# Two casts of the first batch's keys move from VectorE to ScalarE in a fused attention and feed-forward kernel

## The chip, the cores and the metric

One core of one Trainium2 chip. The metric is the time of one execution in microseconds of the device (us), the median over runs. The engines are named as the profile names them: PE is TensorE (matmuls; PEld its weight loads), DVE is VectorE, ACT is ScalarE, POOL is GpSimd, SP is SyncE.

## What is computed

```
a       = softmax(phi)                         # over the last axis, 32 memory slots
k_m     = einsum('bhsm,bhsd->bhmd', a, k)      # 32 summary keys for each head
v_m     = einsum('bhsm,bhsd->bhmd', a, v)
attn    = softmax(q @ k_m^T / sqrt(64))
x       = (attn @ v_m), heads side by side     # 4608 tokens x 512
out     = ((x @ w_a) * (x @ w_b)) @ w_out      # 512 -> 1536 -> 512, float32
```

There are 8 batches of 576 tokens with 8 heads of 64; all inputs and the output are float32. Inside, nearly everything is float16 with float32 sums.

## The kernel before

**Work of one batch.** The keys, values and queries of a batch come as a tile of 128 partitions by 4 head pairs by 576 columns. Exp of phi (ScalarE, L301) is the weight with which TensorE sums keys and values over the tokens (L387 for batch 0, L333 for the others). VectorE scales these sums, TensorE transposes them, and VectorE copies them out as `kvT`. Scores are products of `kvT` with VectorE's 32x32 transposes of the queries (L310, or L316 for batch 1). ScalarE takes exp of them, and sums, logarithm and exp again give the normalised attention `A`.

**Folding.** The values are not multiplied with `A` first. TensorE multiplies the summary values with columns of w_a and w_b (a fold, L526). VectorE or ScalarE copies the result out of PSUM into `vab` (a fold copy, L558). An up-projection is then one product of `vab` with `A` over 256 rows, two matmuls (L738): `a` gives x @ w_a, copied by ScalarE or VectorE (L742), and `b` gives x @ w_b, which VectorE multiplies with it into `ht` (L745). The down-projections of token blocks (L665) follow, in seven products instead of eight.

**The order.** No scheduler places the work. A list of units, `PLAN`, is written out by hand, and each engine gets its instructions in the order in which the units are listed. Each engine works through its own queue in that order and waits by semaphores for the others. The names in the list: `0ks1` are batch 0's key sums of the second half of the heads; `0hv0b` is a fold of batch 0 with a half chunk (256 columns) of w_b, and `0hx0b1` the copy of its second group; `0v1a` is a fold with a whole chunk of 512 columns of w_a; `a0.3.1` is product a of batch 0, output rows 3, second half of the tokens, and `b0.3.1` its partner; `1exp1` is exp of half of batch 1's phi; `1qh10` is a transpose of part of batch 1's queries; `1kv` are batch 1's key and value sums; `2km1` is VectorE's scaling of one group of such sums; `d3` takes the next three steps of the down-projection, a step being one matmul with what belongs to it; `wb512:1024` issues the load of these columns of w_b; `F4` are four filling matmuls on zeros.

**Transfers.** All inputs but one go through GpSimd's queue, which also converts them to float16 on the way. The exception is batch 0's keys. They come as float32 through the queues of SyncE and ScalarE, half each, into room that the tile `ht` lends:

```
L182  k_f32 = ht[:, 0:4].bitcast(F32)
L183  halves = [slice(0, 2), slice(2, 4)]
L184  for engine, x in zip((nc.sync, nc.scalar), halves):
L185      engine.dma_start(out=k_f32[:, x], in_=rows(k, 0)[:, x])
L186  nc.scalar.preload_act_table_set("natural_log_exp_and_others")
```

Two casts, L234 and L235, bring them to float16 in `kv_sb`, each 128 partitions by 1152 columns. They stand ahead of all units of the list. The fold copies of batch 0's half chunks are all VectorE's; this choice and the return of the PSUM bank are here:

```
L553  def take_fold(lo, hi, z, gs=range(2), other=False):
L554      first, second = (x != other for x in (b == 0 and hi <= 512, b < 2))
...
L559          banks.free(bank)
```

Of the kernel before, what the change touches and what calls it, by code (L numbers as in the profile page):

```python
# [17 lines left out]
PLAN = """  # L18
0exp1 F2 wa0:256 wb0:256 wa256:512 F1 M 0ks1 O 0qt1 0kt1 0qt0 wb256:512 0exp0 0ks0 0kt0 0s0 0e0 0qt3 0qt2 0s1 0e1
0den00 p1 0vs0 0den01 0nr00 0den11 0nr11 0den10 0nr10 F1 0vs1 0nr01 0vt0 0vt1 0hv0b 0hx0b0 0hv1a 0hv1b 0hx1b0 0hx1b1  # L20
v1 0hx0b1 0hv0a 0hx1a1 F4 0hx1a0 a0.3.1 1exp1 0hx0a1 a0.2.1 0hx0a0 a0.0.1 b0.0.1 c0.1.0 1exp0 b0.2.1 c0.3.0 b0.3.1
b0.3.0 b0.1.0 c0.0.0 a0.2.0 b0.2.0 b0.0.0 a0.1.1 k1 1kv 1km1 F1 1km0 b0.1.1 1kvt wa512:1024 0v1a 0x1a1 0x1a0 q1.0
1qh10 1qh20 wb512:1024 1qh00 1v1a 1x1a0 1x1a1 1v0a 1v0b a0.4.0 1x0b0 q1.1 1qh30 a0.6.1 a0.6.0 1x0a1 1x0a0 1x0b1
wa1024:1536 1sh0 wb1024:1536 1eh00 0v1b 1eh10 0x1b1 0x1b0 1v1b 1x1b1 1den00 1den10 o0 a0.5.1 b0.4.0 o3 b0.6.0 1qh01
1nr00 1nr10 a0.5.0 a0.7.1 b0.5.0 b0.7.1 1qh31 1x1b0 b0.6.1 a0.4.1 a0.7.0 b0.4.1 a1.2.0 b0.7.0 1qh21 a1.3.0 b1.2.0
a1.4.0 1qh11 a1.1.0 o1 b0.5.1 b1.1.0 a1.0.0 1sh1 1eh01 o4 1eh11 b1.3.0 b1.4.0 o5 0v2a 0x2a0 0x2a1 o2 0v2b a1.6.0 0x2b1
a1.5.0 b1.5.0 0x2b0 1v2a k2 1x2a1 p2 1v2b 1y2b1 a1.7.0 v2 1x2b0 g0.3 b1.6.0 1x2a0 p3 b1.0.0 a0.11.0 c0.10.0 d2 b1.7.0
a0.8.0 b0.8.0 q2 1den01 b0.10.0 b0.11.0 a0.11.1 b0.11.1 T20 1nr01 1den11 V00 a1.9.0 1nr11 a0.9.0 b0.9.0 g0.0 d1
a0.10.1 a0.8.1 a1.11.0 b0.10.1 d1 b1.11.0 a1.5.1 b1.9.0 b1.5.1 b0.8.1 a1.11.1 T10 b1.11.1 d2 T21 a1.10.0 a1.8.0 k3
a0.9.1 v3 b1.8.0 b1.10.0 a1.0.1 b1.0.1 2exp0 a1.6.1 b0.9.1 a1.2.1 V01 a1.1.1 b1.6.1 g0.1 a1.4.1 a1.7.1 b1.4.1 2exp1  # L30
b1.2.1 d3 a1.3.1 V11 T30 d6 2kv d1 g0.2 d2 T31 g1.0 d3 2km1 2km0 d8 a1.10.1 b1.3.1 2kvt d3 3exp0 3exp1 a1.8.1 b1.1.1
2v0a 2x0a1 2qt2 2x0a0 2qt3 2qt0 2qt1 2v1b 2x1b1 2x1b0 g1.1 d7 q3 p5 g1.2 d7 g2.0 q4 d2 2sc d2 2e1 d3 2e0 c1.9.1 b1.9.1
d3 b1.8.1 2den1 d3 h1.3 h2.1 2den0 2nr0 d4 2v1a 2v2b 2x2b1 2y2b0 3kv 3km1 2nr1 d6 3km0 d7 2x1a0 d1 2x1a1 d1 b1.7.1
2v2a v5 2x2a0 2v0b 3qt2 2x0b0 2x0b1 b1.10.1 d2 g2.2 a2.0.0 a2.6.0 b2.6.0 d1 k5 3qt3 2x2a1 d3 3qt1 a2.7.0 a2.2.0 b2.0.0
a2.4.0 d6 v4 d2 3kvt 5exp0 b2.7.0 d2 3qt0 d4 a2.3.0 b2.2.0 3sc 3e0 d2 b2.3.0 3e1 d6 3den0 3nr0 g2.3 a2.1.0 d3 b2.4.0
d3 b2.1.0 a2.5.0 b2.5.0 a2.5.1 a2.8.0 p4 d3 a2.1.1 d3 5exp1 3den1 g4.3 d1 b2.1.1 b2.8.0 a2.9.0 d1 k4 d1 a2.10.1 b2.9.0
a2.4.1 q5 b2.10.1 3nr1 4qt2 3v0b 3v0a 3x0a0 3x0b0 5kv p6 h3.3 b2.5.1 a2.10.0 3x0a1 d2 a2.11.0 a2.9.1 d2 b2.10.0 d1
h3.0 h3.1 h3.2 b2.11.0 b2.9.1 4qt3 d2 3x0b1 a2.0.1 b2.0.1 a2.11.1 b2.4.1 b2.11.1 a2.7.1 b2.7.1 a2.8.1 a2.3.1 a2.2.1
b2.2.1 d2 a3.2.0 a3.3.0 d2 4exp0 b3.2.0 d1 b2.8.1 b3.3.0 d4 4qt1 4exp1 d6 3v2a 3x2a1 4kv 4km1 d5 4km0 3x2a0 a3.0.0 d10
b2.3.1 d1 4qt0 4kvt a2.6.1 b2.6.1 h4.0 a3.3.1 d4 6exp1 d2 5km1 d4 4sc 4e1 d3 4e0 5km0 a3.1.0 h4.1 b3.3.1 d4 a3.0.1  # L40
b3.1.0 h4.2 4ed 4sm0 d1 a3.1.1 d2 5qt0 d1 3v1b 3x1b0 q6 3v2b 3x2b1 5qt1 3v1a d11 3x1a0 d1 b3.0.0 d7 3x1b1 b3.0.1
# [39 lines left out]
def kernel(  # L81
# [11 lines left out]
    nc = tc.nc  # L93
# [51 lines left out]
    kvs = [kv_sbs[b % 2] for b in range(B)]  # L145
# [36 lines left out]
    k_f32 = ht[:, 0:4].bitcast(F32)  # L182
# [49 lines left out]
    make_identity(nc, ident)  # L232
    nc.vector.memset(kv_sbs[0][:, 2], 1.0 / CS)
    for x in halves:  # L234
        nc.vector.tensor_copy(out=kvs[0][:, 0, x], in_=k_f32[:, x])  # L235
    turn = {}

    def tt(engine, **operands):
# [616 lines left out]
```

## Time and profile before

| | us |
|---|---|
| median of three runs | 237.22 |
| lowest and highest | 237.01, 237.41 |
| the profiled execution | 236.62 |
| its span, first to last instruction | 234.70 |
| TensorE busy | 216.0 |
| VectorE busy | 199.3 |
| ScalarE busy | 168.8 |
| GpSimd busy | 148.3 |

The mean granted clock of TensorE over the span is 0.993. A row of the timeline gives the start in us from the span's start, the time in us, the engine (with a q behind it: the queue that issues a transfer), the line, the operation, the tile written and the tiles read, and how many instructions were merged; in brackets stands how long the engine had been idle and what released it. A row of groups gives the form and the count, then busy us and the mean ns of one, then the idle time ahead. A row of issues gives KB and the us from issue to landing. A row of windows gives the stretch, then for each engine busy us and the number of instructions, then granted clock, share of the transfer engines, and GB/s.

### The profile page before, as it was taken

Reading aid. Unit: us, or ns where it says so; the run is one execution under the profiler, and the core shown is the slowest. Engines: PE = TensorE matmul, PEld = TensorE weight load, DVE = VectorE, ACT = ScalarE, POOL = GpSimd, SP = SyncE. Lnnn points to the kernel's source line nnn. Section 1 sums busy time; section 2 is a strip of 40 time slices with the busy share of each in tenths; the row PEclk is TensorE's granted clock in tenths of the full one; section 3 lists DMA queues with packets and bytes.
Section 4 is the critical chain, followed back from the end, with each engine's and each line's share of the span. In section 5 each row is a group of like instructions: output and inputs, shape, how many; then the busy total and the mean of one; then the engine's idle time right before and its main releaser. Section 6 shows DMA issues by size and latency. Waiting matters only on the chain.

```text
span 234.7 us, 7495 instructions
## 1 busy us (share of the span) xinstructions
PE 216.0 (92%) x2906; PEld 164.6 (70%) x2906; DVE 199.3 (85%) x514; ACT 168.8 (72%) x445; POOL 148.3 (63%) x147
## 2 busy tenths in 40 slices
PE   2177989999899999999999999999999999999993
PEld 0133646588587778877777787887778868788882
DVE  3756799999978757789987999998999999999962
ACT  2224459987699998697987988877898679666330
POOL 7685232647785379995867499599474981772201
PEclk9999799999999999999999999999999999999999
DMA  6999999999999999399927632121303213122164
GB/s 229 237 197 258 205 205 205 206 261 256 194 250 217 228 219 245 112 198 253 235 31 164 100 93 67 25 52 43 88 7 89 56 38 91 24 70 67 25 160 110
DMA packets 26259, 34.09 MB, mean 145 GB/s; under 512 B 2000, under 2 KB 20304, under 8 KB 26224
## 3 DMA queue, kind: packets, MB, share of 16 engines
q0 software_dynamic: 19760, 23.14, 54.1%
q1 hardware_dynamic: 5952, 9.70, 15.7%
q10 hardware_dynamic: 512, 0.79, 1.0%
q8 instruction: 22, 0.36, 0.6%
q14 instruction: 13, 0.11, 0.1%
HBM read 42.47 MB, written 9.44 MB: 221 GB/s over the span
## 4 chain that ended last, share of the span: by engine, by line
PE 84%; DVE 9%; ACT 2%; DMA 2%; issue 1%; DVEq 0%
PE py L665 20%; PE pb L738 14%; PE pa L738 14%; PE pv L665 10%; PE pva L526 5%; PE py L761 5%; PE px L665 5%; PE pv L761 3%; DMA ht<-in_k_dram 2%; DVE kv_sb L235 2%; PE pkv L333 2%; DVE vab L558 1%; PE pscore L422 1%; DVE ht L745 1%; PE px L761 1%; PE pk L387 1%
## 5 line engine op out<-in xcount | busy, mean ns | idle before, releaser
L745 DVE TENSOR_TENSOR ht<-a_sb,pb 128x288 f16<-128x288 f16 (+2 forms) x144 | 60.5, 444 | 11.6 <-ACT a_sb L742 4.3
L738 PEld LDWEIGHTS <-vab 128*128 128x128 f16 x576 | 55.9, 99 | 16.2 <-issue 2.2
L742 ACT CAST a_sb<-pa 128x288 f16<-128x288 f32 (+2 forms) x139 | 53.9, 416 | 18.5 <-PE pa L738 15.3
L738 PE MATMUL pa<-A,vab 128*128 128x288 f16 (+2 forms) x288 | 55.2, 290 | 0.5 <-DVE vab L558 0.4
L738 PE MATMUL pb<-A,vab 128*128 128x288 f16 (+2 forms) x288 | 55.0, 287 | 0.1
L558 ACT CAST vab<-pva 128x512 f16<-128x512 f32 x82 | 45.8, 611 | 4.8 <-PE pva L526 4.5
L665 PEld LDWEIGHTS <-h_sums 128*128 128x128 f16 x432 | 41.3, 98 | 9.2 <-issue 2.0
L665 PEld LDWEIGHTS <-ht 128*128 128x128 f16 x324 | 31.3, 98 | 7.3 <-issue 2.1
L665 PE MATMUL py<-w_sums,h_sums 128*128 128x256 f16 x216 | 35.5, 273 | 0.0
L665 PE MATMUL pv<-wo_sb,h_sums 128*128 128x256 f16 x216 | 34.5, 273 | 0.0
L240 POOL TENSOR_TENSOR h_sums<-ht 128x768 f16<-128x768 f16 x17 | 27.7, 1642 | 8.1 <-DVE ht L745 3.7
L766 ACT COPY z<-py 128x288 f32<-128x288 f32 x48 | 19.4, 416 | 6.5 <-PE py L761 4.6
L240 POOL TENSOR_TENSOR ht<-ah,bh 128x288 f16<-128x288 f16 x20 | 14.3, 731 | 11.8 <-DVE ah L770 8.7
L665 PE MATMUL py<-wo_sb,ht 128*128 128x256 f16 x108 | 18.4, 273 | 0.0
L665 PE MATMUL px<-wo_sb,ht 128*128 128x256 f16 x108 | 18.3, 273 | 0.0
L665 PE MATMUL py<-w_sums,ht 128*128 128x256 f16 x108 | 17.8, 273 | 0.0
L672 ACT ACTIVATE u<-py 128x256 f32<-128x256 f32 x36 | 14.6, 404 | 4.5 <-PE py L665 4.0
L435 ACT ACTIVATE E<-pscore 128x288 f16<-128x288 f32 x28 | 9.6, 418 | 7.7 <-PE pscore L422 7.5
L240 POOL TENSOR_TENSOR h_sums<-h_sums,ht 128x768 f16<-128x768 f16 x8 | 13.1, 1640 | 3.1 <-DVE h_sums L240 2.7
L301 ACT ACTIVATE exp_sb<-phi_sb 128x576 f16<-128x576 f32 x16 | 10.8, 694 | 5.2 <-DMA phi_sb<-in_phi_dram 5.2
L240 POOL TENSOR_TENSOR h_sums<-ht,h_sums 128x768 f16<-128x768 f16 x8 | 13.1, 1643 | 0.2
L761 PE MATMUL py<-asum,vab 128*128 128x288 f16 x48 | 13.1, 286 | 0.0
(107 smaller groups left out, 401.8 us busy)
## 6 DMA issues: line engine op xcount, KB each, us to landing
out_dram<-o_sb SPq DMA_DIRECT2D x68, 128.0 KB, 2.4
phi_sb<-in_phi_dram POOLq DMA_DIRECT2D x8, 576.0 KB, 8.0
kv_sb<-in_v_dram POOLq DMA_DIRECT2D x8, 576.0 KB, 9.9
kv_sb<-in_k_dram POOLq DMA_DIRECT2D x7, 576.0 KB, 10.7
q_sb<-in_q_dram POOLq DMA_DIRECT2D x6, 576.0 KB, 9.6
wo_sb<-in_moe_w_out_dram POOLq DMA_DIRECT2D x6, 256.0 KB, 14.0
wa_sb<-in_moe_w_a_dram POOLq DMA_DIRECT2D x2, 512.0 KB, 15.4
wb_sb<-in_moe_w_b_dram POOLq DMA_DIRECT2D x2, 512.0 KB, 17.4
```

The costliest lines, as they stand in the source:

```text
L240: x = engine.tensor_tensor(**operands)
L301: nc.scalar.activation(out=t["exp"][:, 2 * z:2 * z + 2, :, :], in_=phis[b][:, 2 * z:2 * z + 2, :].rearrange("p c (i m) -> p c i m", m=M), ...
L435: nc.scalar.activation(out=Ev[:, g, :, z, :], in_=pss, func=AF.Exp, scale=1.0 / (8.0 * CS))
L526: nc.tensor.matmul(t["pva", lo, z][g][0][32 * j:32 * j + 32, 0:hi - lo], t["kvT"][64 * r:64 * r + 64, 4 + g if side else 2, M * j:M * j + ...
L558: engine_copy(out=vabs[b][z][:, g, lo:hi], in_=pva[:, 0:hi - lo])
L665: nc.tensor.matmul(po, lhs[:, i], rhs[:, i], start=first and i == 0, stop=i == KH - 1, skip_group_check=not first)
L672: nc.scalar.mul(out=x, in_=po, mul=scale)
L738: nc.tensor.matmul(ps, vabs[b][x][:, g, P * i:P * (i + 1)], attn[b][:, g, ts], start=(g == 0), stop=(g == 1))
L742: engine_copy(out=a_sbs[b, i, hf][:, :n], in_=ps)
L745: nc.vector.tensor_tensor(out=ht[:, i, t0:t0 + n], in0=a_sbs.pop((b, i, hf))[:, :n], in1=ps, op=ALU.mult)
L761: nc.tensor.matmul(x[bank][0], lhs, rhs, start=first, stop=True, skip_group_check=True)
L766: engine_copy(out=x[name], in_=po)
```

## The change

The two casts of batch 0's keys become ScalarE copies. In ScalarE's queue they stand behind the table load and ahead of the two exp instructions of batch 0. On VectorE nothing stands in their place.

Three units of the list are at another place: `0hx0b1` from ahead of `0hv0a` to behind `1exp1`, so behind `a0.3.1`; `a1.1.0` from behind `1qh11` to ahead of `a1.3.0`; `2km1` one step of the down-projection forward. The other changed lines of the list only break elsewhere. On the engines this gives: ScalarE two instructions more and VectorE two fewer at the start, one fold copy two places further back on VectorE, and two matmuls of `a1.1.0` six matmuls further ahead on TensorE. GpSimd and SyncE keep their order.

```
-v1 0hx0b1 0hv0a 0hx1a1 F4 0hx1a0 a0.3.1 1exp1 0hx0a1 a0.2.1 0hx0a0 a0.0.1 b0.0.1
+v1 0hv0a 0hx1a1 F4 0hx1a0 a0.3.1 1exp1 0hx0b1 0hx0a1 a0.2.1 0hx0a0 a0.0.1 b0.0.1
...
-1qh21 a1.3.0 b1.2.0 a1.4.0 1qh11 a1.1.0 o1
+1qh21 a1.1.0 a1.3.0 b1.2.0 a1.4.0 1qh11 o1
...
-g1.0 d3 2km1 2km0 d8
+g1.0 d2 2km1 d1 2km0 d8
...
     for x in halves:
-        nc.vector.tensor_copy(out=kvs[0][:, 0, x], in_=k_f32[:, x])
+        nc.scalar.copy(out=kvs[0][:, 0, x], in_=k_f32[:, x])
```

More of the change, by code (lines that the diff above doesn't have):

```diff
@@ L20 @@
 0den00 p1 0vs0 0den01 0nr00 0den11 0nr11 0den10 0nr10 F1 0vs1 0nr01 0vt0 0vt1 0hv0b 0hx0b0 0hv1a 0hv1b 0hx1b0 0hx1b1
-v1 0hx0b1 0hv0a 0hx1a1 F4 0hx1a0 a0.3.1 1exp1 0hx0a1 a0.2.1 0hx0a0 a0.0.1 b0.0.1 c0.1.0 1exp0 b0.2.1 c0.3.0 b0.3.1
+v1 0hv0a 0hx1a1 F4 0hx1a0 a0.3.1 1exp1 0hx0b1 0hx0a1 a0.2.1 0hx0a0 a0.0.1 b0.0.1 c0.1.0 1exp0 b0.2.1 c0.3.0 b0.3.1
 b0.3.0 b0.1.0 c0.0.0 a0.2.0 b0.2.0 b0.0.0 a0.1.1 k1 1kv 1km1 F1 1km0 b0.1.1 1kvt wa512:1024 0v1a 0x1a1 0x1a0 q1.0
@@ L24 @@
 wa1024:1536 1sh0 wb1024:1536 1eh00 0v1b 1eh10 0x1b1 0x1b0 1v1b 1x1b1 1den00 1den10 o0 a0.5.1 b0.4.0 o3 b0.6.0 1qh01
-1nr00 1nr10 a0.5.0 a0.7.1 b0.5.0 b0.7.1 1qh31 1x1b0 b0.6.1 a0.4.1 a0.7.0 b0.4.1 a1.2.0 b0.7.0 1qh21 a1.3.0 b1.2.0
-a1.4.0 1qh11 a1.1.0 o1 b0.5.1 b1.1.0 a1.0.0 1sh1 1eh01 o4 1eh11 b1.3.0 b1.4.0 o5 0v2a 0x2a0 0x2a1 o2 0v2b a1.6.0 0x2b1
+1nr00 1nr10 a0.5.0 a0.7.1 b0.5.0 b0.7.1 1qh31 1x1b0 b0.6.1 a0.4.1 a0.7.0 b0.4.1 a1.2.0 b0.7.0 1qh21 a1.1.0 a1.3.0
+b1.2.0 a1.4.0 1qh11 o1 b0.5.1 b1.1.0 a1.0.0 1sh1 1eh01 o4 1eh11 b1.3.0 b1.4.0 o5 0v2a 0x2a0 0x2a1 o2 0v2b a1.6.0 0x2b1
 a1.5.0 b1.5.0 0x2b0 1v2a k2 1x2a1 p2 1v2b 1y2b1 a1.7.0 v2 1x2b0 g0.3 b1.6.0 1x2a0 p3 b1.0.0 a0.11.0 c0.10.0 d2 b1.7.0
@@ L30 @@
 a0.9.1 v3 b1.8.0 b1.10.0 a1.0.1 b1.0.1 2exp0 a1.6.1 b0.9.1 a1.2.1 V01 a1.1.1 b1.6.1 g0.1 a1.4.1 a1.7.1 b1.4.1 2exp1
[L31 to L38, printed above, removed]
+b1.2.1 d3 a1.3.1 V11 T30 d6 2kv d1 g0.2 d2 T31 g1.0 d2 2km1 d1 2km0 d8 a1.10.1 b1.3.1 2kvt d3 3exp0 3exp1 a1.8.1
+b1.1.1 2v0a 2x0a1 2qt2 2x0a0 2qt3 2qt0 2qt1 2v1b 2x1b1 2x1b0 g1.1 d7 q3 p5 g1.2 d7 g2.0 q4 d2 2sc d2 2e1 d3 2e0 c1.9.1
+b1.9.1 d3 b1.8.1 2den1 d3 h1.3 h2.1 2den0 2nr0 d4 2v1a 2v2b 2x2b1 2y2b0 3kv 3km1 2nr1 d6 3km0 d7 2x1a0 d1 2x1a1 d1
+b1.7.1 2v2a v5 2x2a0 2v0b 3qt2 2x0b0 2x0b1 b1.10.1 d2 g2.2 a2.0.0 a2.6.0 b2.6.0 d1 k5 3qt3 2x2a1 d3 3qt1 a2.7.0 a2.2.0
+b2.0.0 a2.4.0 d6 v4 d2 3kvt 5exp0 b2.7.0 d2 3qt0 d4 a2.3.0 b2.2.0 3sc 3e0 d2 b2.3.0 3e1 d6 3den0 3nr0 g2.3 a2.1.0 d3
+b2.4.0 d3 b2.1.0 a2.5.0 b2.5.0 a2.5.1 a2.8.0 p4 d3 a2.1.1 d3 5exp1 3den1 g4.3 d1 b2.1.1 b2.8.0 a2.9.0 d1 k4 d1 a2.10.1
+b2.9.0 a2.4.1 q5 b2.10.1 3nr1 4qt2 3v0b 3v0a 3x0a0 3x0b0 5kv p6 h3.3 b2.5.1 a2.10.0 3x0a1 d2 a2.11.0 a2.9.1 d2 b2.10.0
+d1 h3.0 h3.1 h3.2 b2.11.0 b2.9.1 4qt3 d2 3x0b1 a2.0.1 b2.0.1 a2.11.1 b2.4.1 b2.11.1 a2.7.1 b2.7.1 a2.8.1 a2.3.1 a2.2.1
 b2.2.1 d2 a3.2.0 a3.3.0 d2 4exp0 b3.2.0 d1 b2.8.1 b3.3.0 d4 4qt1 4exp1 d6 3v2a 3x2a1 4kv 4km1 d5 4km0 3x2a0 a3.0.0 d10
```

## The prediction

> **What bounds the kernel now.** I read the page first, then the chain of waits of the first 70 us, then the timeline of that stretch engine by engine, the transfers with their landings, and busy time by windows.
>
> ```profile
> span 234.7 us, 7495 instructions
> PE 216.0 (92%) x2906; PEld 164.6 (70%) x2906; DVE 199.3 (85%) x514; ACT 168.8 (72%) x445; POOL 148.3 (63%) x147
> ...
> 36.00:234.70 198.70, 193.60 (x2468) 152.85 (x2466) 175.16 (x456) 155.24 (x413) 127.65 (x116) 1.00 0.63 131
> ```
>
> The last row is busy time after 36 us: TensorE works 193.60 of 198.70 us (97%). From there on it sets the time, it takes its instructions in the order of the list, and whatever its start is moved by, the end is moved by nearly as much. Before 36 us it is 216.0 - 193.6 = 22.4 us busy in 36: that stretch has 13.6 us of idle time. The chain of waits (start, us, what) says what it waited for:
>
> ```profile
> 0.81 4.95 DMA ht<-in_k_dram
> ...
> 5.79 4.64 DVE kv_sb L235 x2
> ...
> 10.57 1.17 PE pk L387 x34
> ...
> 21.86 2.09 DVE vab L558 x6
> ...
> 24.00 0.67 PE pa L738 x2
> ```
>
> Batch 0's keys land at 5.76, two VectorE casts (L235, the instructions that the change moves) take 4.64 us with nothing else on the chain, and 0.14 us later the first sums of keys start (10.57). At 24.00 the first up-projection starts behind six fold copies. The casts are dear because of their neighbour; three rows of the timeline, by engine:
>
> ```profile
> 5.79 2.07 DVE L235 CAST kv_sb<-ht 128x1152 f16<-128x1152 f32 x1 [2.38 <-DMA ht<-in_k_dram]
> 7.78 2.65 DVE L235 CAST kv_sb<-ht 128x1152 f16<-128x1152 f32 x1
> 7.22 2.59 POOL L803 MEMSET kv_sb<- 128x2304 f16 x1
> ```
>
> GpSimd issues transfers until 7.22 and then fills a tile until 9.81. The second cast ends 0.62 us after that fill (10.43), the first 0.64 us after the issues (7.86): each looks like 0.6 us of work behind a wait for GpSimd. The Trainium skill says so (SBUF — State Buffer, "SBUF: two separate sides"): VectorE in its two-port mode and GpSimd hold one port pair in turn, each blocking the other for a whole instruction. These ends agree.
>
> **The casts on ScalarE.** It is free: after its table load it waits for batch 0's phi and does the two halves of exp from 7.81 to 9.07. The casts now stand ahead of those in its queue. No row has ScalarE casting 1152 columns; the nearest, by shape (mean ns of one):
>
> ```profile
> 1.34 1.28 ACT L186 ACT_TABLE_LOAD   x1 [1.34 <-PEq L839]
> ...
> 7.81 1.26 ACT L301 ACTIVATE exp_sb<-phi_sb 128x576 f16<-128x576 f32 x2 [5.19 <-DMA phi_sb<-in_phi_dram]
> ...
> L558 ACT CAST vab<-pva 128x512 f16<-128x512 f32 x82 | 45.8, 611 | 4.8 <-PE pva L526 4.5
> ...
> L486 ACT ACTIVATE vsum<-asum 128x576 f16<-128x576 f32 x4 | 2.8, 688 | 0.1
> L486 ACT ACTIVATE vsum<-asum 128x288 f16<-128x288 f32 x4 | 1.7, 436 | 0.1
> ```
>
> From 288 to 576 columns, same types, same memory, the price grows by 252 ns; 576 columns more make 688 + 504 = 1192 ns. Bounds: twice the 576-column instruction, 1376; the CAST scaled up by columns, 1375; below, the 620 ns that VectorE needs unblocked. I take 1.19, by the row of the same memory. Casts 5.79 + 2.38 = 8.17; the half of exp that comes first 0.68 (half of 1.26 with its overlap, rounded up) to 8.85; plus the 0.14 above: the sums start at 8.99, **1.58 us earlier**. The second half of exp would end at 9.5; its reader, the second sums of keys, would come at 12.64 - 1.58 = 11.06:
>
> ```profile
> 12.64 1.15 PE L387 MATMUL pk<-kv_sb,exp_sb 64*32 64x128 f16 x36
> ```
>
> A rule of the Trainium skill speaks against the change (ScalarE: Activation LUTs, "Rules for kernel authors"): plain elementwise work belongs on VectorE, up to about three times faster per element. By it alone the two casts would cost 1.24 us on VectorE (0.62 each) against 2.38, so the change would lose 1.1 us here; the row of 4.64 us decides against it, since VectorE isn't free of GpSimd.
>
> Moved with it: VectorE has nothing from 3.4 us until the sums are done. GpSimd's two mask instructions wait for a VectorE memset behind those sums, and eight transfer issues stand behind them in its queue; all go some 1.6 us sooner. That brings no data sooner: the 16 DMA engines are full and serve that queue in order.
>
> ```profile
> DMA  6999999999999999399927632121303213122164
> ...
> 12.47 0.31 POOL L270 TENSOR_SCALAR_AFFINE_SELECT ones<-ones 128x128 f16<-128x128 f16 x1 [2.66 <-DVE ones L269]
> ...
> 15.33 0.78 POOL L152 DMA_DIRECT2D kv_sb<-in_k_dram  x1
> 16.06 0.79 POOL L174 DMA_DIRECT2D wa_sb<-in_moe_w_a_dram  x1
> 16.79 0.80 POOL L171 DMA_DIRECT2D q_sb<-in_q_dram  x1
> 17.52 0.81 POOL L174 DMA_DIRECT2D wb_sb<-in_moe_w_b_dram  x1
> ...
> kv_sb<-in_k_dram POOLq DMA_DIRECT2D x1, 576.0 KB, 11.9
> ...
> wa_sb<-in_moe_w_a_dram POOLq DMA_DIRECT2D x1, 512.0 KB, 13.6
> wb_sb<-in_moe_w_b_dram POOLq DMA_DIRECT2D x1, 512.0 KB, 16.4
> q_sb<-in_q_dram POOLq DMA_DIRECT2D x1, 320.0 KB, 14.6
> ```
>
> Issue plus time to landing: batch 1's keys 27.2, the second 512 columns of w_a 29.7, the early part of batch 1's queries 31.4, the second 512 columns of w_b 33.9. I hold these fixed. They are where the gain is cut.
>
> **The three list moves.** `0hx0b1` (one of eight fold copies) goes behind the first up-projection:
>
> ```profile
> 21.86 2.74 DVE L558 CAST vab<-pva 128x256 f16<-128x256 f32 x8 [0.41 <-PE pva L526]
> ```
>
> One copy is 2.74 / 8 = 0.34 us. Five stand ahead of the first product instead of six: 0.34 more, so 24.00 becomes 24.00 - 1.58 - 0.34 = 22.08. The moved copy is needed only by a later product that waits for the same eight copies as before. `a1.1.0` goes ahead of three products on TensorE; the four need the same folds, so TensorE's sum is unchanged, and each of the three comes one pair of matmuls (some 0.27 us) later into a full VectorE queue: 0, at worst 0.27. `2km1` passes one step of the down-projection that is only a matmul, and the order on every engine stays the same: 0. New waits (GpSimd's later load of the kv buffer on ScalarE, two VectorE products on the transfers of the keys) are for things done 20 us earlier: 0.
>
> **The sum, gate by gate.** The consumers of the four landings, now (start, us):
>
> ```profile
> 28.96 0.94 PE L333 MATMUL pkv<-kv_sb,exp_sb 64*32 64x192 f16 x72
> ...
> 31.57 0.41 PE L526 MATMUL pva<-wa_sb,vsum 64*32 64x512 f16 x8
> ...
> 32.69 0.79 DVE L316 STREAM_TRANSPOSE qT<-q_sb 128x160 f32<-128x160 f32 x3
> ...
> 34.87 0.47 PE L526 MATMUL pva<-wb_sb,vsum 64*32 64x512 f16 x8
> ```
>
> Shift 1.92 puts 28.96 at 27.04, the keys land at 27.2: shift 1.7. 31.57 - 1.7 = 29.87, the weights are there (29.7): 1.7. 32.69 - 1.7 = 31.0, the queries land at 31.4: 1.3. 34.87 - 1.3 = 33.57, the weights land at 33.92: **0.95**. TensorE takes its list in order, so all behind this fold is 0.95 earlier and no more. The later landings leave more room; the tightest that I found is batch 2's phi, which lands at 40.87 + 11.5 = 52.4 and is first read at 53.94:
>
> ```profile
> 40.87 0.75 POOL L149 DMA_DIRECT2D phi_sb<-in_phi_dram  x1 [1.86 <-ACT a_sb L742]
> ...
> phi_sb<-in_phi_dram POOLq DMA_DIRECT2D x1, 576.0 KB, 11.5
> ...
> 53.94 0.69 ACT L301 ACTIVATE exp_sb<-phi_sb 128x576 f16<-128x576 f32 x1
> ```
>
> At 97% busy TensorE carries the shift to the end. The profiled execution took 236.62 us (span 234.70 and 1.92 around it): 235.67. The three runs have their median at 237.22, 0.60 above the profiled one; against it 236.27, so **236.3 us**. The forecast hardly depends on the ScalarE price: up to 1.68 us a cast the 0.95 stands; the gain is gone only at 2.15 ((10.57 + 0.34 - 5.79 - 0.68 - 0.14) / 2). Its own range is 235.9 to 236.8: 0.27 and small collisions on one side, some of TensorE's remaining 5.1 us of idle time on the other.
>
> **Rivals.**
>
> (1) The landings come sooner too. The Trainium skill has a rule to that end (SBUF — State Buffer, "SBUF: two separate sides"): a VectorE fp32 copy keeps GpSimd from writing descriptors, so transfers starve. Here, freed issues would pull the four landings along, no gate would bind, and 1.7 to 1.9 us would remain: 235.4. Against it: GpSimd's issues under the cast take as long as the others, and the DMA line is at nine tenths from the second slice on. Chance 0.06.
>
> ```profile
> 5.76 0.75 POOL L174 DMA_DIRECT2D wb_sb<-in_moe_w_b_dram  x1
> 6.49 0.76 POOL L174 DMA_DIRECT2D wa_sb<-in_moe_w_a_dram  x1
> ```
>
> (2) The gain is eaten: the last gate moves later (the four wait 11.9 to 16.4 us in the queue, and 0.95 is little beside that), or VectorE and ScalarE fall behind in the dense stretch. Then 236.9 to 237.3, with 237.1 in the middle. For it: four landings in a row each cut something. Against it: their order is unchanged. Chance 0.12.
>
> (3) Slower, through TensorE's clock. The windows (PE busy first, granted clock after POOL's column):
>
> ```profile
> 19.66:23.08 3.42, 1.99 (x44) 0.94 (x44) 2.54 (x10) 0.99 (x3) 1.49 (x2) 0.99 1.20 210
> 23.08:26.49 3.41, 2.98 (x13) 1.60 (x12) 1.71 (x6) 1.79 (x5) 0.70 (x1) 0.51 1.22 209
> ...
> 29.90:33.31 3.41, 2.70 (x42) 1.08 (x43) 3.29 (x13) 1.11 (x2) 1.40 (x2) 1.00 1.33 207
> ```
>
> A stretch with 1.99 us of work in 3.42 was followed by one at half clock. The Trainium skill names it (TensorE: Matmul & The Clock Gate, "What's actually happening"): windows of 3.4 us, half rate after an idle one. In the changed kernel, TensorE comes early to 28 us and waits there for landings: the 2.70 us of work in 29.90 to 33.31 is stretched by up to 1.7 - 0.95 = 0.75, which leaves about 1.95, as little as before the drop. If the clock falls then, 3.41 us at half rate lie where TensorE is full, and 1.7 us of work is lost against 0.95 gained: 237.22 + 0.75 = 238.0. It decides from some 2 us of work in a window. Against it: the stretch also takes in the front of the next work (scores, the folds), which by my placing leaves 2.6. Chance 0.12. By the same rows the half-rate stretch at 23 us may vanish; the landings behind it would take that gain away.
>
> **How the numbers follow.** Forecast 0.70, rivals 0.06, 0.12, 0.12. A measurement here tells about 0.2% (0.47 us) from no change: faster is below 236.75, slower above 237.69. Faster: nearly all of the forecast, 0.69, and rival 1: 0.75. Same: rival 2 and the forecast's edge, 0.13. Slower: rival 3, 0.12. The range takes in rival 1, the forecast and the better part of rival 2: 235.3 to 237.2, leaving out 0.12 above and some 0.05 of rival 2.
>
> **What would show it.** In the changed kernel's profile: ScalarE CASTs from 5.8 of 1.1 to 1.4 us; the first matmul on the keys near 9.0; the first up-projection near 22.1; key sums of batch 1 near 27.2, w_a's second fold 29.8, query transposes 31.4, w_b's second fold 33.9 to 34.0, each with a DMA as its releaser; a granted clock of 1.00 after 27 us; everything behind 0.9 to 1.0 earlier. It is wrong if casts of over 2 us, a landing that moved, or half clock after 30 us shows.

## The result and the profile after

The changed kernel takes **234.99 us** (median; 234.68 to 235.54), beside it the kernel before 237.31: ratio 0.9900, 95% interval 0.9879 to 0.9921. Forecast were 236.3 us and a range of 235.3 to 237.2: the direction was right, the time lies below the range, and the gain of 2.3 us is more than twice the 0.95 that I foresaw. The profiled execution took 235.11 us (before 236.62). Its page:

```profile
span 233.1 us, 7498 instructions
...
PE 216.7 (93%) x2906; PEld 164.6 (71%) x2906; DVE 194.6 (83%) x512; ACT 170.8 (73%) x447; POOL 147.8 (63%) x147
```

Its busy time after 36 us, by windows:

```profile
36.00:233.10 197.10, 192.20 (x2461) 152.09 (x2459) 174.16 (x454) 153.90 (x410) 127.49 (x115) 1.00 0.63 133
```

VectorE lost 4.7 us of busy time and ScalarE gained 2.0. TensorE's work is the same, and behind 36 us it is as full as before (97.5%). So most of the gain is a shift of its start. The chain of waits (start, us, what):

```profile
0.81 5.05 DMA ht<-in_k_dram
5.89 2.21 ACT kv_sb L235 x2
8.10 0.59 ACT exp_sb L301
...
8.73 1.18 PE pk L387 x28
...
19.46 1.33 PE pva L526 x29
20.79 1.84 PE pw L229 x4
...
22.67 1.60 PE pa L738 x6
```

The 4.64 us of casts are 2.21, the sums of keys start at 8.73 instead of 10.57, and the first product at 22.67 instead of 24.00. Ahead of it the chain has a new piece, the four filling matmuls (`F4`, L229, 1.84 us). In the timeline these are the points to compare:

```profile
7.22 2.06 POOL L803 MEMSET kv_sb<- 128x2304 f16 x1
...
22.10 0.11 PEld L738 LDWEIGHTS <-vab 128*128 128x128 f16 x1 [0.40 <-DVE vab L558]
...
27.75 0.94 PE L333 MATMUL pkv<-kv_sb,exp_sb 64*32 64x192 f16 x72
...
30.37 0.41 PE L526 MATMUL pva<-wa_sb,vsum 64*32 64x512 f16 x8
31.49 0.79 DVE L316 STREAM_TRANSPOSE qT<-q_sb 128x160 f32<-128x160 f32 x3
...
33.95 0.95 ACT L465 ACTIVATE E<-pscore 128x160 f16<-128x160 f32 x4
34.11 0.11 PEld L526 LDWEIGHTS <-vsum 64*32 64x32 f16 x8 [0.59 <-DMA wb_sb<-in_moe_w_b_dram]
34.11 0.41 PE L526 MATMUL pva<-wb_sb,vsum 64*32 64x512 f16 x8 [0.43 <-ACT vab L558]
...
34.67 0.58 PE L475 MATMUL pD<-E,ones 128*128 128x320 f16 x2
34.95 0.30 PE L475 MATMUL pD<-E,ones 128*128 128x320 f16 x1
```

The last row is the second of the two matmuls by itself. Batch 1's sums start 1.21 us earlier than before, w_a's fold and the query transposes 1.20. The fold of w_b's second 512 columns waits for its transfer, as forecast, and is only 0.76 earlier. But `pD`, the denominators behind it in TensorE's list, is 1.20 earlier (35.87 before, below), and so is exp of the scores that `pD` reads. So in this execution the late fold holds nothing that matters.

GpSimd's memset (L803) took 2.59 us beside VectorE's casts and takes 2.06 with the casts on ScalarE.

### The profile page after: what moved, and what is told of

It reads as the page before. It is cut to its first block, busy times and chain, and to the rows that moved or that the text cites. A ratio compares the mean times of both kernels' runs of the same rounds, so it can differ in the third digit from the quotient of the medians.

```text
span 233.1 us, 7498 instructions
## 1 busy us (share of the span) xinstructions
PE 216.7 (93%) x2906; PEld 164.6 (71%) x2906; DVE 194.6 (83%) x512; ACT 170.8 (73%) x447; POOL 147.8 (63%) x147
## 4 chain that ended last, share of the span: by engine, by line
PE 88%; DVE 4%; ACT 3%; DMA 2%; issue 1%; DVEq 0%; ACTq 0%
PE py L665 20%; PE pa L738 15%; PE pb L738 15%; PE pv L665 10%; PE pva L526 6%; PE py L761 5%; PE px L665 5%; PE pv L761 3%; DMA ht<-in_k_dram 2%; PE pkv L333 2%; PE pscore L422 1%; PE px L761 1%; PE pk L387 1%; PE pD L475 1%; DVE h_sums L240 1%; ACT kv_sb L235 1%
## 5 line engine op out<-in xcount | busy, mean ns | idle before, releaser
L310 DVE STREAM_TRANSPOSE qT<-q_sb 128x288 f32<-128x288 f32 x28 | 12.3, 457 | 0.0
```

The lines of the kernel that those rows point to most:

```text
L310: nc.vector.transpose(out=t["qT"][:, hp, :].bitcast(F32), in_=qs[b][:, hp, :].bitcast(F32))
```

## The experiments

The theory: VectorE's casts wait for GpSimd; without that wait all of the first stretch is earlier, and TensorE carries it to the end, one for one. The rivals: the landings hold it at 0.95, as my sum has it; the list moves bring part; TensorE's clock does it. Ratios are to the kernel before, with 95% intervals.

**The kernel before again.**

> The kernel before, once more, to see how far its executions differ and with what clock of TensorE. The profiled execution of before was 236.62 us, under all six timed ones (237.01 to 238.29), while that of the changed kernel (235.11) lies among its own (234.68 to 235.54). Theory A: the 0.7 us between them is TensorE's clock; before has one half-clock stretch at 23.1 to 26.5 us (mean clock 0.993) in its profile, and more or a worse placed one in most executions, so time and clock go together: runs at 0.993 near 236.6, runs at 0.985 near 237.4. Rival B: the clock is the same in all of them and the time differs for another reason; then spans of 235.1 to 235.5 stand beside 0.993.

No edit. Measured: 1.0005 (0.9985 to 1.0025), median 236.91. Its executions, and those of the same kernel beside it, have spans of 234.2 to 235.8 us (median 234.9) at mean clocks of 0.989 to 1.000, in no order: 234.2 and 235.8 both stand at 1.000, 234.6 at 0.992. The mean clock doesn't explain which of them are short, against theory A. The profiled execution that I predicted from, with its 234.7, lies in the lower part of this scatter.

**The casts alone.**

> The two casts on ScalarE, the list as in before. Theory A: the casts carry all of it. The first sums of keys start at 8.73 as in the changed kernel, and the earlier place of 0hx0b1 is worth nothing, since in the changed kernel the first up-projection waited for the four filling matmuls (end 22.6) and not for the fold copies (LDWEIGHTS at 22.10): with six copies ahead it would start at 22.4 to 22.7. 234.8 to 235.3 us. Rival B: the list moves carry 0.3 us (one fold copy) or more: 235.3 to 235.8.

```
 for x in halves:
-    nc.vector.tensor_copy(out=kvs[0][:, 0, x], in_=k_f32[:, x])
+    nc.scalar.copy(out=kvs[0][:, 0, x], in_=k_f32[:, x])
```

Measured: 0.9934 (0.9914 to 0.9953), 235.16 us, median span 233.05 against 235.0 beside it. The casts bring most of the gain: 1.95 us of span, for sums that start 1.71 us earlier in its profile (8.86).

**The list moves alone.** Of each line of the list only a part is shown, here and in the edits below.

> The three list moves, the casts on VectorE. Theory A: at most one fold copy (0.34 us) is won at 24.0 us, and the filling matmuls, which end at 23.57 in before, leave about that: 236.9 to 237.4. Rival B (moves matter, or do harm without the casts): 236.3 or less, or 237.8 or more.

```
-v1 0hx0b1 0hv0a 0hx1a1 F4 0hx1a0 a0.3.1 1exp1 0hx0a1
+v1 0hv0a 0hx1a1 F4 0hx1a0 a0.3.1 1exp1 0hx0b1 0hx0a1
...
-1qh21 a1.3.0 b1.2.0 a1.4.0 1qh11 a1.1.0 o1
+1qh21 a1.1.0 a1.3.0 b1.2.0 a1.4.0 1qh11 o1
...
-g1.0 d3 2km1 2km0 d8
+g1.0 d2 2km1 d1 2km0 d8
```

Measured: 1.0017 (0.9998 to 1.0036). With the casts on VectorE the moves bring nothing.

**VectorE keeps its casts, and GpSimd's fill goes later.** `M` is the GpSimd memset at L803.

> The kernel before, casts on VectorE, but GpSimd's fill of the second kv buffer (2.59 us, 7.22 to 9.81) is put behind the load of batch 1's phi, some 6 us later. Theory A: the casts cost 0.62 us each and wait for GpSimd; without the fill the first ends at 7.86 as before, the second at 8.5, the sums of keys start at 8.6 (exp ends at 8.45), and all gains as much as with ScalarE: 234.8 to 235.5. Rival B: a cast of this shape costs VectorE 2.1 to 2.6 us by itself: sums at 10.5, time as before, 237.0 to 237.6.

```
-F1 M 0ks1 O 0qt1
+F1 0ks1 O 0qt1
...
-p1 0vs0
+p1 M 0vs0
```

Measured: 0.9921 (0.9893 to 0.9949), 234.94 us: the gain of the change with no cast on ScalarE. Its timeline:

```profile
5.75 1.07 POOL L174 DMA_DIRECT2D wb_sb<-in_moe_w_b_dram  x1
5.76 1.62 DVE L235 CAST kv_sb<-ht 128x1152 f16<-128x1152 f32 x2 [2.35 <-DMA ht<-in_k_dram]
...
8.53 1.15 PE L387 MATMUL pk<-kv_sb,exp_sb 64*32 64x128 f16 x36 [5.80 <-ACT exp_sb L301]
...
12.57 2.04 POOL L803 MEMSET kv_sb<- 128x2304 f16 x1
```

The casts of this kernel, and below them those of the changed kernel, by source line (ns, min/median/max):

```profile
L235 DVE CAST kv_sb<-ht x2: 760/852/944, 5.8 to 6.4; 128x1152 f16<-128x1152 f32 x2
```

```profile
L235 ACT CAST kv_sb<-ht x2: 1147/1150/1152, 5.9 to 6.9; 128x1152 f16<-128x1152 f32 x2
```

With only transfer issues beside them, VectorE's two casts are through in 1.62 us instead of 4.64; ScalarE needs 2.21. So most of the 4.64 was waiting, and both ways of keeping the casts clear of the fill bring the gain. The Trainium skill says of VectorE and GpSimd that whichever holds their shared port pair blocks the other for a whole instruction (SBUF — State Buffer, "SBUF: two separate sides"): the trace agrees for the memset, 2.65 us for a cast beside it and 0.76 to 0.94 without.

The first cast is another matter. The prediction read its 2.07 us as a wait for the transfer issues, and the expectation had it end at 7.86 again. Here an issue starts 0.01 us ahead of it, and yet the cast takes 0.76 us and the issue 1.07 instead of 0.75. So the issues alone don't hold a cast. Why the first one waited until the fill began stays open.

**The changed kernel again, and without `F4`.**

> The changed kernel once more, beside the next three on one chip. In the two profiles TensorE stands 1.83 us earlier at the sums of keys, 1.33 at the first up-projection, 1.20 from 28 us on and 1.5 at the end, while the medians lie 2.0 to 2.3 apart. Theory A: the change is worth about as much as the start moves, 1.8 to 2.0, and the two profiled executions understate it: median 234.9 to 235.2. Rival B: it is worth 1.2 to 1.5 and the first six runs were lucky: 235.4 to 235.8.

Measured: 0.9899 (0.9880 to 0.9917), 234.80 us; the spans are 232.5 to 233.2, median 232.9. In its profile the sums of keys start at 9.19 instead of 8.73, since exp waits 0.37 us for batch 0's phi. Yet the first product starts at 22.30, 0.37 sooner than in the first profile, because `F4` takes less time there (below).

> The changed kernel without the four filling matmuls F4 ahead of the first up-projection (their results are not used). In its profile they ran at half clock, 0.63 us each, and ended at 22.61, while the weights of the first up-projection were loaded from 22.10. Theory A: the fill takes 0.57 us of the gain; without it the first product starts at 22.1 and all behind it gains up to 0.5: 234.4 to 234.8, if no landing cuts it. Rival B: the landings cut it (second chunk of w_b at 34.1 in that profile): 234.9 to 235.2. Rival C: the fill is what brings the clock up, and without it half clock lasts one window longer: 235.5 to 236.5.

```
-v1 0hv0a 0hx1a1 F4 0hx1a0 a0.3.1
+v1 0hv0a 0hx1a1 0hx1a0 a0.3.1
```

Measured: 0.9911 (0.9889 to 0.9933), 234.93 us: the same time, within rival B's. TensorE's timeline at the first product, of the first profile of the changed kernel, of the repeat, and of the kernel without `F4`:

```profile
20.72 1.89 PE L229 MATMUL pw<-warm 128*128 128x512 f16 x4
22.67 1.60 PE L738 MATMUL pa<-A,vab 128*128 128x288 f16 x6
```

```profile
20.97 1.24 PE L229 MATMUL pw<-warm 128*128 128x512 f16 x4 [0.21 <-DVE vab L558]
22.30 1.65 PE L738 MATMUL pa<-A,vab 128*128 128x288 f16 x6
```

```profile
21.78 1.65 PE L738 MATMUL pa<-A,vab 128*128 128x288 f16 x6 [1.54 <-DVE vab L558]
```

The four filling matmuls take 1.89 us in the first profile and end at 22.61, half a microsecond after the first weights are loaded (22.10); in the repeat they take 1.24 us, and in the third there are none and the product starts at 21.78. Yet the times agree: in the kernel without `F4` the query transposes start at 31.08, 0.02 after their transfer's landing, the fold of w_b at 33.61, 0.04 after its landing, and `pD` at 34.27, against 34.36 in the repeat.

**The kernel before without `F4`.**

> The kernel before without F4. There the fill ended 0.4 us ahead of the last fold copy that the first product needs. Theory A: it costs before nothing, so taking it away gives 236.8 to 237.1. Rival C: it brings the clock up: 237.5 to 238.5.

Measured: 1.0023 (1.0003 to 1.0043), 237.58 us, as rival C has it. There the fill is worth a little: without it the products run at 444 ns each until 28.1 us, and at 286 ns after that; with it they reach 286 ns at 26.5 us.

**More casts on the chain.** The casts of the changed kernel are done twice (four casts), or only the second one is (three).

> The changed kernel with each of the two ScalarE casts done twice, one behind the other: 2.2 us more on the chain ahead of the sums of keys, which then start near 10.9 instead of 8.73 (10.57 in before). Theory A: nothing between 9 and 36 us takes up such a shift, each microsecond at the start is one at the end: 237.0 to 237.3. Rival B, the gates of the forecast: the landings hold the later stages in any case, so that only 1.0 to 1.3 comes through: 235.9 to 236.4.

```
     for x in halves:
         nc.scalar.copy(out=kvs[0][:, 0, x], in_=k_f32[:, x])
+        nc.scalar.copy(out=kvs[0][:, 0, x], in_=k_f32[:, x])
```

> The changed kernel with the second of its two casts done twice: 1.1 us more ahead of the sums of keys, half of what doing both twice added (2.45 us in time for 2.2 us). Theory A: one for one over the whole stretch: 235.9 to 236.2. Rival B: the landings hold the changed kernel back and the first part of a delay is free: 235.0 to 235.5.

```
     for x in halves:
         nc.scalar.copy(out=kvs[0][:, 0, x], in_=k_f32[:, x])
+    nc.scalar.copy(out=kvs[0][:, 0, halves[1]], in_=k_f32[:, halves[1]])
```

The first sums in the timeline, of four casts and of three:

```profile
11.22 1.04 PE L388 MATMUL pk<-kv_sb,exp_sb 64*32 64x128 f16 x32 [8.49 <-ACT exp_sb L302]
```

```profile
10.17 1.15 PE L388 MATMUL pk<-kv_sb,exp_sb 64*32 64x128 f16 x36 [7.43 <-ACT exp_sb L302]
```

Measured: 1.0015 (0.9996 to 1.0035), 237.25 us, with four; 0.9944 (0.9925 to 0.9964), 235.72 us, with three. Against the changed kernel (sums at 8.73, ratio 0.9899) that is 2.75 us for 2.49 us of delay (the ratios' difference by 237 us), and 1.07 us for 1.44, each uncertain by some 0.6. Against the repeat's profile (sums at 9.19) the delays are 2.03 and 0.98. The 235.72 us of three casts lie between the two theories' ranges. The prediction said that "up to 1.68 us a cast the 0.95 stands". Three casts are 3.45 us, as long as two of 1.73, so nearly nothing of the gain should have gone. Nearly half of it went.

**The fill later, with the list moves.**

> Casts on VectorE, GpSimd's fill put later, and the three list moves. With the fill put later alone the sums of keys start at 8.53, 0.2 ahead of the changed kernel, and wait for exp of phi. Theory A: this is as good as the changed kernel, and the list moves add nothing that can be told: 234.5 to 235.0. Rival B: the moves add a fold copy's 0.3: 234.2 to 234.6.

The edits are those of the moves alone and of the later fill. Measured: 0.9925 (0.9904 to 0.9946), against 0.9921 without the moves: they bring nothing here either. The median of 235.21 us is above the ranges of both theories.

**Two gates taken away**, in the changed kernel.

> The changed kernel, in which the fold of the second 512 columns of w_b reads the first 512 columns for batches 0 and 1, so that it doesn't wait for the transfer that lands at 33.8 to 34.1 (the results of those columns differ). Theory A: this landing is not on the path; TensorE waits for it and has time for that ahead of the next scores' sums: time as the changed kernel, 234.6 to 235.1. Rival B, the last gate of the forecast: all behind the fold comes up to 0.6 earlier: 234.1 to 234.4.

```
-    w_sbs[z][64 * r:64 * r + 64, hp, lo:hi],
+    w_sbs[z][64 * r:64 * r + 64, hp, slice(0, 512) if z and lo == 512 and b < 2 else slice(lo, hi)],
```

Measured: 0.9904 (0.9880 to 0.9928), 235.03 us. TensorE's timeline:

```profile
33.62 0.49 PE L526 MATMUL pva<-wb_sb,vsum 64*32 64x512 f16 x8
...
34.63 0.57 PE L475 MATMUL pD<-E,ones 128*128 128x320 f16 x2
```

The fold no longer waits and starts at 33.62 instead of 34.11. `pD` starts at 34.63 instead of 34.67. Half a microsecond at the gate is worth 0.04 behind it, and nothing that the times can tell (their ratios are uncertain by 0.6 us).

> The changed kernel, in which the transposes of the early part of batch 1's queries read batch 0's query tile, so that they don't wait for the transfer that lands at 30.8 to 31.1 (the results of those tokens differ). Theory A: the landing binds only in executions where the stage before comes early (transposes at 31.08 right behind it where F4 is left out, at 31.17 to 31.49 in the two profiles of the changed kernel): 0 to 0.3 us gained, 234.5 to 234.9. Rival B: it is the gate of every execution: 234.0 to 234.4.

```
-    def q_part(b, hf):
+    def q_part(b, hf, of=None):
...
-        flat = qs[b].rearrange("p c t -> p (c t)")
+        flat = qs[b if of is None else of].rearrange("p c t -> p (c t)")
...
-            nc.vector.transpose(out=t["qT"][:, hp, ts].bitcast(F32), in_=q_part(b, hf)[:, hp].bitcast(F32))
+            nc.vector.transpose(out=t["qT"][:, hp, ts].bitcast(F32), in_=q_part(b, hf, 0 if hf == 0 else b)[:, hp].bitcast(F32))
```

Measured: 0.9899 (0.9877 to 0.9921), 234.69 us: nothing again. In its profile the queries land at 30.80 and the transposes start at 31.09, so in that execution the wait would not have held them; the test rests on the times alone.

## Where the prediction was right, and where it failed

**The casts: right.** They were waiting for GpSimd's fill; the later fill shows it by itself. That the first of them waited for the transfer issues did not come out. ScalarE's price was 1.15 us against 1.19 forecast. The sums start at 8.73, 0.26 sooner than forecast: 0.07 from the end of the casts, 0.09 from the half of exp (0.59, not 0.68), and 0.10 from the 0.14 that I had put between exp and sums and that is 0.04.

**One fold copy less: right in size.** From the first fold copy to the first product it is 2.14 us before (21.86 to 24.00) and 1.80 in the repeat of the changed kernel (20.50 to 22.30): 0.34, as forecast.

**The fills: not costed.** I took the fold copies for the only wait ahead of the first product. The first weights were loaded at 22.10, forecast 22.08, but `F4` held TensorE until 22.61. So the shift in that profile is 1.84 at the sums and 1.33 at the first product, and it is 1.20 from 28 us on. Without `F4` it is 2.2 there, cut to 1.6 at `pD` (34.27): where the shift is largest, landings do cut, since the transposes and the fold start right behind theirs. But it is 1.86 again at the next denominators, of the kernel before and of the changed kernel without `F4`:

```profile
46.86 0.27 PE L475 MATMUL pD<-E,ones 128*128 128x256 f16 x1
```

```profile
45.00 0.27 PE L475 MATMUL pD<-E,ones 128*128 128x256 f16 x1
```

**The gates: the step that failed.** "34.87 - 1.3 = 33.57, the weights land at 33.92: **0.95**. TensorE takes its list in order, so all behind this fold is 0.95 earlier and no more." The landing is close to where I put it (34.07), and the fold waited for it: its row above also names a copy of ScalarE, but in the run without the wait the fold starts at 33.62 while that copy still runs. The conclusion is false because TensorE had room behind that fold: `pD` reads ScalarE's exp of the scores. The timeline of the kernel before, behind the fold at 34.87:

```profile
35.36 0.58 PE L526 MATMUL pva<-wb_sb,kvT 64*32 64x512 f16 x8
35.87 0.59 PE L475 MATMUL pD<-E,ones 128*128 128x320 f16 x2
36.16 0.30 PE L475 MATMUL pD<-E,ones 128*128 128x320 f16 x1
...
35.16 0.95 ACT L465 ACTIVATE E<-pscore 128x160 f16<-128x160 f32 x4
```

ScalarE's exp begins at 35.16 and `pD` 0.71 later; in the changed kernel 33.95 and 0.72 later. The second matmul of `pD` starts 0.05 behind the end of exp in both (36.16 and 34.95). These distances are the same, while the fold moved by less: from fold to `pD` it is 1.00 us before and 0.56 after, so the fold before had 0.44 us of room. By these rows, as an estimate, a landing at 33.92 lets `pD` start at 33.92 + 0.04 + 0.56 = 34.52, a shift of 1.35 and not of 0.95. That the late fold has room also shows in the run without the wait. The added casts say the same of the gates together: they cost about one for one, within their uncertainty. Had the gates made the first 0.97 us of a delay free (1.92 less 0.95), four casts would have lost 1.5 us and not 2.75. The other three gates were also too late in my sum: the keys, w_a's chunk and the queries landed at 26.75, 29.29 and 30.98, against 27.2, 29.7 and 31.4. But the unchanged kernel's second profile has 27.11, 29.39 and 31.08, so a good part of this is what one execution differs from the next; "held fixed" was finer than these times are known.

In the profiles the step is worth 0.25 us: behind the fold the shift is 1.20 and not 0.95, and it is still 1.20 at 57 us. The span is 1.6 us shorter. So 0.4 more came later, where I had let TensorE carry the shift on unchanged. Some 0.3 of it lies behind the last sums of keys and values (162.62 and 161.32). From these sums to the end the profiles of this case take 71.7 to 72.5 us, so that part is within their scatter.

**From profile to median: half of the miss.** The sum gave 235.67 for the profiled execution, which took 235.11: 0.56 too much. I then added 0.60, since before's profile lay 0.60 below its median; after's lies 0.12 above: 0.72 more. The spans of single executions tell why. Before, they have a median of 235.0 and the profile 234.7; in the repeat of the changed kernel the median is 232.9 and the profiles have 233.1 and 233.2. So the medians of the spans differ by 2.1 us and the profiled executions by only 1.6, since one was a short one of its kernel and the others rather long ones. What lies around the span is the same (medians 1.9 to 2.0). The spans of one kernel scatter by 0.5 to 2.0 us, so two profiles cannot settle half a microsecond. My sum without the gates was 1.92; with the 0.26 of the earlier sums it is 2.18, and 237.22 - 2.18 = 235.04, against 234.99 measured. That agreement is of a sum with a median. It does not show that each term is passed on whole in each execution: in the profile `F4` took some of it. What makes the spans scatter stays open; the clock in the first 28 us (below) and the landings differ from one execution to the next, and neither was tried by itself.

**The rivals.** (1) came nearest in time (235.4) but not by its mechanism: issues went 1.1 to 1.8 us sooner (batch 1's keys 13.50 instead of 15.33) and three of the four landings some 0.4, of which for two of them 0.3 also lie between two profiles of the unchanged kernel; and of the gates it would have moved, the two that were taken away are worth nothing that the times can tell. (2) and (3) did not occur: the granted clock stays at 1.00 from 25.4 us to the end of the work. (3) had its stretch nearly as placed, with 2.6 to 2.7 us of work in 3.4, above the 1.99 at which the clock fell.

**The list moves: 0, not refuted.** Nothing is shown for them with VectorE's casts, alone or with the later fill. With ScalarE's casts the ratio is 0.9934 without and 0.9899 with them, and the intervals touch. By the median spans (233.05 and 232.9) it is 0.15 us; more is possible, and nothing is shown.

## What to carry to other kernels

Before a landing or a late producer is made a bound, look at what stands behind its reader: only if that reader's successor isn't waiting for something later does the delay pass on. A cast that takes far longer than its size explains may be waiting for a neighbour (here 4.64 us for two against 1.62); in this kernel moving the neighbour, one list unit, and moving the casts bring the same. And a forecast from one profile carries the distance of that profile from the median twice, once for each kernel: put it into the range, not into the sum.

## What the runs showed of the hardware

**Filling matmuls take two thirds longer where the clock is at half.** The same four, with the one of `F1` ahead of them, took these times (ns) in the changed kernel and in its repeat, where the 634 is that one:

```profile
L229 PE MATMUL pw<-warm x5: 609/634/634, 16.5 to 22.0; 128*128 128x512 f16 x5
```

```profile
L229 PE MATMUL pw<-warm x5: 376/384/634, 16.9 to 21.6; 128*128 128x512 f16 x5
```

The windows of both (PE's busy time first, granted clock after POOL's column), changed kernel, then repeat, in steps of 3.41 us back from where the products change from 444 to 286 ns (25.38 and 25.05):

```profile
15.15:18.56 3.41, 2.84 (x81) 1.66 (x80) 0.91 (x4) 2.95 (x10) 1.35 (x2) 1.00 1.43 234
18.56:21.97 3.41, 2.81 (x39) 1.13 (x40) 2.83 (x11) 0.29 (x1) 1.92 (x3) 1.00 1.14 259
21.97:25.38 3.41, 3.35 (x14) 1.79 (x13) 1.51 (x6) 2.04 (x5) 1.00 (x2) 1.00 1.21 207
```

```profile
14.82:18.23 3.41, 3.29 (x97) 1.67 (x81) 0.59 (x2) 2.95 (x10) 2.14 (x3) 1.00 1.45 209
18.23:21.64 3.41, 1.97 (x48) 1.00 (x44) 2.53 (x10) 1.04 (x3) 1.72 (x3) 1.00 1.15 282
21.64:25.05 3.41, 3.32 (x14) 1.56 (x13) 2.05 (x7) 2.05 (x5) 1.20 (x2) 0.50 1.22 209
```

In the changed kernel two stretches with 2.84 and 2.81 us of work did not raise the clock, the next with 3.35 did. In the repeat 3.29 raised it, and 1.97 lowered it again. Which stretch is full enough depends on where it begins, and that differs between executions: the boundaries are at 25.38 in the one and at 25.05 in the other, with the same kernel. The Trainium skill describes free-running windows of 3.4 us (TensorE: Matmul & The Clock Gate, "What's actually happening"); the trace agrees with that length, and adds how full they were.

**The clock column has nothing before the first change that was recorded.** It shows 1.00 in the changed kernel until 25.38, where products take 444 ns; the repeat has 0.50 beside products of that length. So that profile's mean clock of 1.000 against 0.993 before is no gain in clock.
